# One core, long-convolution block: the forward and the inverse table product that share a matrix go into one matmul of 256 columns, the cosine products go to GpSimd, and the hand-written order is drawn up anew

## The chip, the core and the metric

The kernel runs on one core of one Trainium2 chip. A core has five engines with a queue each, and each runs its queue strictly in order: TensorE (PE: matmuls, and PEld for the weight loads in front of them), VectorE (DVE), ScalarE (ACT), GpSimd (POOL) and SyncE (SP, which only issues transfers here). Engines wait for each other through semaphores. The metric is device time in microseconds (us) of one execution, lower is better.

## The reference, cut to what matters

The program is a sequence of two residual blocks on a 2048 x 512 input:

```python
h  = x + A(layernorm(x))        # A: a state-space convolution
h2 = h + B(layernorm(h))        # B: a gated MLP over tokens

def A(u):                       # u: (1, L=2048, D=512), N=128 states per channel
    dt = exp(log_dt); A = -exp(log_A_real) + 1j*A_imag; C = (C_real + 1j*C_imag)*dt[:, None]
    P  = exp((A*dt[:, None])[:, :, None] * arange(L))
    K  = 2.0*einsum("dn,dnl->dl", C, P).real          # one filter of length L per channel
    y  = irfft(rfft(K, 2*L) * rfft(u.T, 2*L))[:, :L]  # convolution by FFT of length 4096
    return y.T + u*D_skip

def B(x):
    z = gelu(x @ w_in); z1, z2 = split(z)
    return (z1 * (w_sp @ layernorm(z2) + b_sp)) @ w_out
```

The change touches only A: how the filters K are generated, and how they and the input go through the transform.

## The kernel before, in words

**Stages.** The program has four parts, one after the other: phase A (`phase_a`, the convolution), then `phase_b1`, `phase_b2` and `phase_b3` (block B). Phase A works through the 512 channels in four chunks of 128 (`NCH`); each chunk is cut into eight pieces of 16 channels. All its arithmetic is float32.

**A unit** (`unit`, L481; 32 of them, eight per chunk) generates the filters of 16 channels as a sum over the 128 states. PE makes phases from a table (`ps<-c_k,sw`), ACT and DVE reduce them (`wb<-ps,wb`, `wb<-wb,ps`), ACT takes the sine of both halves (`ps<-wb` of 1024 columns), the absolute value, and the cosine of both halves (two activations of 512 columns: `ce`, and `cw`, L499 to L501). POOL makes three products of decay tables (`wa<-mt`). DVE makes the three sine products (`f<-ps,wa`, `f<-wa,ps`) and the `ce` product (`wa<-ps,wa`, 1024 columns). The `cw` product is made on DVE for odd units (`wb<-ps,wa`, with `cw` in a PSUM bank) and on POOL for even ones (`wb<-wb,wa`, with `cw` in SBUF), by `EVERY = 2`. PE then sums over the states in two rounds of 16 small matmuls (`ps<-f` and `ps<-wa,wb`), and ACT or DVE copies the result to one of six buffers `ks`.

**The tables** of decays (`table`, L471) are made for a half of a chunk: POOL multiplies (`mt<-rcs,wb`), ACT takes an exponential (`mt<-mt`), POOL multiplies once more. The exponential needs another function table in ACT than sine does, so ACT loads a table ahead of it and the sine's table again behind it (`ACT_TABLE_LOAD`).

**The transform** of a chunk has five kinds of pieces:
- a (`piece_a`): first step of the transform of the input (weights `big` or `wa`, moving `c_f` in `wb`); the result goes to `x1us`, that is `trio[1]` for chunk 0 and `big[2]` for the others.
- b (`piece_b`): second step. For each of 32 frequencies a matrix of the table `a2` (`a` in the profile) is the stationary operand, and 128 columns of `x1us` move. Four frequencies fill a PSUM bank; ACT or DVE copies it to the spectrum in `trio` (`trio<-ps`, 512 columns).
- c (`piece_c`): the first step for the filters of a unit (weights `ks`); the result goes to `x1k`, that is `big[3]`.
- d (`piece_d`): the second step for the filters, with the same 32 matrices of `a2`. DVE multiplies the result into the spectrum (`trio<-ps,trio`, 1024 columns: the PSUM bank is read for two planes). For chunks 0 to 2 there are eight groups of four matrices with 128 columns; for chunk 3 the 32 lanes are cut in two halves (`split`, L645), so that there are two times four groups of eight matrices with 64 columns.
- e (`piece_e`): the inverse step (weights `trio`, moving `c_inv`), copied to `big`, from which block B begins (matmuls `y<-big,g`).

`exchange(c)` swaps the halves of a spectrum with two transfers (`trio<-trio`), after the inverse step of chunk c-1 has read them.

**What sets the order.** In phase A nothing is issued as it is written. Every operation is recorded by `Plan`; the string `RANKS` gives each a rank, `FORMS` chooses between two engines where `either` leaves the choice (mostly PSUM copies on ACT or DVE), `BANKS` names the PSUM bank. Then all are issued by rank from one helper, which is why they all have the line L250, each engine's queue in that order. A matmul in float32 stands as two records in the profile.

## Time and profile before

| what | value |
|---|---|
| median of 3 runs | 848.29 us (847.11 to 849.35) |
| the profiled execution: its own time | 844.69 us |
| its span | 842.9 us, granted clock 0.999 |
| busy over the span | PE 794.1 us, PEld 685.6 us, DVE 654.2 us, ACT 469.1 us, POOL 278.5 us |
| last copy of phase A starts | 296.76 us |
| first matmul of block B starts | 297.40 us |

The span is what the engines show from their first instruction to their last; the execution's own time is 1.8 us more. "Busy" is the union of an engine's instructions. For PE that includes their pipeline: records overlap, so what one costs is the length of a run of records divided by their number, not the mean of one. A group's row in the profile ends with the engine's idle time ahead of it and what ended that.

### The profile page before, as it was taken

The numbers are of one execution on the slowest core, as the hardware profiler recorded it, in microseconds if no ns is written. First come the engines' busy times: TensorE is split into PE (matmuls) and PEld (weight loads), VectorE is DVE, ScalarE is ACT, GpSimd is POOL, SyncE is SP. The second block draws the span as 40 slices with busy tenths as digits, with TensorE's granted clock in tenths as the row PEclk, the third lists the DMA queues.
The fourth block names the chain that finished last, engine by engine and source line by source line (L and its number), as shares of the span: only waits on it lengthen the run. The fifth ranks groups of instructions, "written<-read, shape, count | busy, mean of one in ns | idle before, by whom it ended". The sixth has DMA issues, their size and how long they took to land.

```text
span 842.9 us, 17463 instructions
## 1 busy us (share of the span) xinstructions
PE 794.1 (94%) x6813; PEld 685.6 (81%) x6813; DVE 654.2 (78%) x1260; ACT 469.1 (56%) x783; POOL 278.5 (33%) x332
## 2 busy tenths in 40 slices
PE   1388999999998999999999999999999999999998
PEld 0287889899997998888899988888887888888886
DVE  7999998999999488851367679988955985787633
ACT  5998999999897233543223345456534533454111
POOL 5778777787755000000042100324221002222200
PEclk9999999999999999999999999999999999999999
DMA  9231432302218676364175044899889558799832
GB/s 352 76 113 32 111 91 61 86 25 62 52 38 269 233 251 163 99 172 154 51 150 126 1 126 132 187 228 213 201 206 210 171 149 189 156 236 216 204 110 77
DMA packets 63875, 121.81 MB, mean 145 GB/s; under 512 B 6737, under 2 KB 21201, under 8 KB 61489
## 3 DMA queue, kind: packets, MB, share of 16 engines
q1 hardware_dynamic: 52160, 99.33, 38.9%
q0 software_dynamic: 11632, 21.37, 15.6%
q8 instruction: 53, 0.87, 0.4%
q14 instruction: 30, 0.24, 0.1%
HBM read 92.89 MB, written 19.40 MB: 133 GB/s over the span
## 4 chain that ended last, share of the span: by engine, by line
PE 67%; DVE 14%; DMA 7%; issue 6%; ACT 5%; POOL 1%; SPq 1%; DVEq 0%; ACTq 0%; POOLq 0%
PE ps L250 20%; PE m L1140 18%; PE pz L835 9%; PE pz L935 9%; DMA raws<-in_w_sp_dram 6%; PE po L1063 5%; DVE trio L250 4%; PE y L748 3%; PE pl L1063 2%; ACT wb L250 2%; DVE wts L676 1%; ACT big L250 1%; ACT ps L250 1%; DVE wb L250 1%; DVE f L250 1%
## 5 line engine op out<-in xcount | busy, mean ns | idle before, releaser
L1140 PE MATMUL m<-wts,zc_wa 128*128 128x512 f32 x700 | 218.0, 391 | 1.0 <-DVE c L1155 1.0
L1140 PEld LDWEIGHTS m<-wts,zc_wa 128*128 128x128 f32 x700 | 131.4, 188 | 29.8 <-DVE c L1155 1.5
L1140 PE MATMUL m<-wts,zc_wb 128*128 128x512 f32 x350 | 136.7, 391 | 0.0
L1011 POOL DMA_DIRECT2D raws<-in_w_sp_dram x64 | 58.1, 1009 | 209.2 <-DMA raws<-in_w_sp_dram 208.0
L250 POOL TENSOR_TENSOR wa<-mt 128x512 f32<-128x512 f32 x96 | 107.3, 1131 | 35.2 <-PE ps L250 15.6
L675 ACT CAST wts<-raws 128x512 fp32r<-128x512 f32 x112 | 68.8, 619 | 52.3 <-DMA raws<-in_w_sp_dram 31.7
L676 DVE TENSOR_TENSOR wts<-raws,wts 128x512 fp32r<-128x512 f32 x112 | 77.0, 690 | 19.6 <-ACT wts L675 19.5
L935 PE MATMUL pz<-w,ht 128*128 128x448 f32 x384 | 77.4, 363 | 0.0
L1140 PEld LDWEIGHTS m<-wts,zc_wb 128*128 128x128 f32 x350 | 65.7, 188 | 14.0
L935 PEld LDWEIGHTS pz<-w,ht 128*128 128x128 f32 x384 | 72.0, 188 | 5.3
L835 PE MATMUL pz<-ht,w1h 128*128 128x512 f32 x224 | 71.3, 395 | 0.0
L250 ACT ACTIVATE ps<-wb 128x512 f32<-128x512 f32 (+1 forms) x80 | 65.3, 825 | 3.4 <-DVE trio L250 1.3
L941 POOL TENSOR_SCALAR sm<-sm 128x1 f32<-128x1 f32 x16 | 5.5, 342 | 186.3 <-DVE sm L940 186.3
L250 PE MATMUL ps<-big,a 128*128 128x128 f32 (+1 forms) x512 | 62.4, 278 | 0.9 <-DVE trio L250 0.8
L675 ACT CAST zc_wa<-raws 128x384 fp32r<-128x384 f32 (+1 forms) x70 | 37.0, 533 | 46.8 <-DVE raws L1045 34.1
L1063 PE MATMUL po<-w,gz 128*128 128x512 f32 x252 | 62.6, 396 | 0.0
L250 PEld LDWEIGHTS ps<-big,a 128*128 128x128 f32 x512 | 59.3, 192 | 3.5 <-DVE trio L250 1.1
L250 PE MATMUL ps<-c_inv,trio 128*128 128x128 f32 x512 | 60.6, 277 | 1.3 <-DVE trio L250 1.3
L250 PEld LDWEIGHTS ps<-c_inv,trio 128*128 128x128 f32 x512 | 58.8, 192 | 3.2 <-DVE trio L250 1.9
L1063 PEld LDWEIGHTS po<-w,gz 128*128 128x128 f32 x252 | 47.3, 188 | 11.5 <-DVE zo L1103 0.4
L835 PEld LDWEIGHTS pz<-ht,w1h 128*128 128x128 f32 x224 | 42.1, 188 | 9.2
L1045 DVE TENSOR_TENSOR raws<-z 128x384 f32<-128x384 f32 (+1 forms) x80 | 46.1, 584 | 0.3
(162 smaller groups left out, 1533.0 us busy)
## 6 DMA issues: line engine op xcount, KB each, us to landing
raws<-in_w_sp_dram SPq DMA_DIRECT2D x112, 256.0 KB, 4.0
raws<-in_w_sp_dram POOLq DMA_DIRECT2D x80, 256.0 KB, 5.8
trio<-trio SPq DMA_DIRECT2D x8, 1024.0 KB, 6.9
g<-in_c_g_dram SPq DMA_DIRECT2D x8, 1024.0 KB, 6.7
scr_z<-zo SPq DMA_DIRECT2D x28, 256.0 KB, 2.3
big<-in_u_a_dram SPq DMA_DIRECT2D x8, 512.0 KB, 7.6
xq<-in_u_b_dram SPq DMA_DIRECT2D x4, 1024.0 KB, 6.7
scr_h<-xq SPq DMA_DIRECT2D x16, 256.0 KB, 4.9
```

Of the source, the lines that this page charges most:

```text
L250: r = getattr(getattr(self.nc, e), method)(*map(self.real, args), **{k: self.real(x) for k, x in kw.items()})
L675: nc.scalar.copy(hi, src)
L676: nc.vector.tensor_sub(lo, src, hi.bitcast(F32))
L748: nc.tensor.matmul(ys[n, g][:, i, :], gt[:, i, r, :], qv[:, r, l0 + i], start=(r == 0), stop=(r == 1))
L835: nc.tensor.matmul(pt, w[:, q, f], ht[n][k][:, q], start=(q == 0 and i == 0), stop=(q == 3 and i == 2))
L935: nc.tensor.matmul(pt[:, :FQ], a[:, q], w2[:, b, q, f], start=(q == 0 and i == 0), stop=(q == 3 and i == 2))
L941: nc.gpsimd.tensor_scalar_add(sm[:, 14:15], sm[:, 13:14], 1e-5)
L1011: nc.gpsimd.dma_start(r, ws[1], accum_op=ALU.add)
L1045: nc.vector.tensor_tensor(zs[:, :w], x, y, op=op)
L1063: nc.tensor.matmul(pt, gz[fb][x][:, P * a:P * a + P], wo[:, y, fb, w], start=(first and fb == fbs[0] and i == 0), stop=(last and fb == fbs ...
L1140: nc.tensor.matmul(pt, x[:, f], y, start=(k == 0 and i == 0), stop=(k == KT - 1 and i == 2))
```

## The change

Phase A alone is changed, in four places.

1. Piece b of chunk c+1 and piece d of chunk c become one piece `piece_bd(c, g)` for c = 0, 1, 2: one matmul per frequency with 256 moving columns (128 of `x1us` and 128 of `x1k`, which lie side by side in `big[2:4]`). Two frequencies fill a bank, so there are 16 groups in place of 8 + 8; each group is emptied by one copy of 256 columns (ACT or DVE) and one DVE product of 512 columns. `piece_b` stays for chunk 0, `piece_d` for chunk 3. To fit, `x1us` takes the layout of `x1k`.
2. Chunk 3's piece d is no longer cut in halves: eight groups of four matrices with 128 columns, as the other chunks had.
3. The `cw` product is made on POOL for all units; `cw` stays in SBUF.
4. `RANKS`, `FORMS` and `BANKS` are new strings.

```diff
-            ce, cw = nc.bank([P, 1, W], 0), nc.bank([P, W], 0) if su % EVERY == 1 % EVERY else cs[:, 0, :]
-            nc.scalar.activation(ce, cs[:, 1:2, :], AF.Sin, bias=half_pi, scale=-TWO_PI)
-            nc.scalar.activation(cw, cs[:, 0, :], AF.Sin, bias=half_pi, scale=-TWO_PI)
+        ce, cw = nc.bank([P, 1, W], 0), cs[:, 0, :]
+        nc.scalar.activation(ce, cs[:, 1:2, :], AF.Sin, bias=half_pi, scale=-TWO_PI)
+        nc.scalar.activation(cw, cs[:, 0, :], AF.Sin, bias=half_pi, scale=-TWO_PI)
...
-        if su % EVERY == 1 % EVERY:
-            nc.vector.tensor_mul(cs[:, 0, :], cw, m[:, 2, :])
-        else:
-            nc.gpsimd.tensor_tensor(cw, cw, m[:, 2, :], op=ALU.mult)
+        nc.gpsimd.tensor_tensor(cw, cw, m[:, 2, :], op=ALU.mult)
         with nc.group():
-            product(cs[:, 0, :], m[:, 0:2, :], 1)
+            product(cw, m[:, 0:2, :], 1)
...
-    x1us = [x.rearrange("p (k d q) -> p k d q", k=NK1, q=4) for x in (trio[:, 1], big[:, 2, :])]
+    x1us = [x.rearrange("p (k q d) -> p k q d", k=NK1, q=4) for x in (trio[:, 1], big[:, 2, :])]
+    x1b = big[:, 2:4, :].rearrange("p i (k q d) -> p i k q d", k=NK1, q=4)
...
+    def piece_bd(c, g):
+
+        pt = bank("s2", [P, 2, 32, 2, 4])
+        with nc.group():
+            for j in range(2):
+                nc.tensor.matmul(pt[:, :, :, j, :].rearrange("p i d q -> p i q d"), a2v[:, 2 * g + j, :], x1b[:, :, 2 * g + j, :, :],
+                                 start=True, stop=True)
+        o = spectra(c + 1)[0][:, :, 2 * g:2 * g + 2, :]
+        nc.either(lambda: nc.scalar.copy(o, pt[:, 0]), lambda: nc.vector.tensor_copy(o, pt[:, 0]))
+        v = spectra(c)[2].rearrange("p i (d k) -> p i d k", d=32)[:, :, :, 8 * g:8 * g + 8]
+        nc.vector.tensor_mul(v, pt[:, 1].rearrange("p d k q -> p d (k q)").unsqueeze(1).to_broadcast([P, 2, 32, 8]), v)
...
         if c + 1 < NCH:
             pieces(piece_a, c + 1)
-            pieces(piece_b, c + 1)
-        split = [(0, 32)] if c + 1 < NCH else [(0, 16), (16, 16)]
-        for lo, m in split:
-            for g in range(NK1 // (1 << (P // m).bit_length() - 1)):
-                piece_d(c, g, lo, m)
-            for s in range(lo // 4, (lo + m) // 4):
-                piece_e(c, s)
+        for g in range(16 if c + 1 < NCH else 8):
+            if c + 1 < NCH:
+                piece_bd(c, g)
+            else:
+                piece_d(g)
+        for s in range(8):
+            piece_e(c, s)
```

Of the three strings one line each shows the kind of change:

```diff
-    "05000608010709040B0F0A0R0M0V0I0f0Z0j03020C0E0G0H0J0K0L0O0Q0S0U0X0Y0a0N0b0d0m0g0l0o0r0u0z10121316181A1D1Y1O1a1d1h1t221w25"
+    "07000504010Q060B0A0F0I090M080b0k0W0g03020C0E0G0H0J0K0L0N0O0R0U0V0Z0c0Y0d0e0m0i0l0p0r0v0y0z0-11121416191K1U1X1r1p1w252629"
```

What they do to the queues shows at three places. The first is the end of phase A on PE: the last pieces of chunk 3 (c from `ks`, d from `big,a`, e from `c_inv`). Before:

```order
L250 MATMUL ps_101<-big,a_78 128x4x16 x8
L250 MATMUL ps_100<-big,a_78 128x4x16 x8
L250 MATMUL ps_103<-big,a_78 128x4x16 x8
L250 MATMUL ps_98<-big,a_78 128x4x16 x8
L250 MATMUL ps_102<-f_94 32x64 x16
L250 MATMUL ps_102<-wa,wb 32x64 x16
L250 MATMUL ps_100<-f_95 32x64 x16
L250 MATMUL ps_100<-wa,wb 32x64 x16
L250 MATMUL ps_102<-wb,ks_80 64x128 x8
L250 MATMUL ps_100<-wb,ks_81 64x128 x8
L250 MATMUL ps_101<-c_inv,trio 128x128 x8
L250 MATMUL ps_103<-c_inv,trio 128x128 x8
```

and at the same place now, from the last two units on:

```order
L250 MATMUL ps_101<-f_94 32x64 x16
L250 MATMUL ps_101<-wa,wb 32x64 x16
L250 MATMUL ps_103<-wb,ks_85 64x128 x8
L250 MATMUL ps_99<-wb,ks_80 64x128 x8
L250 MATMUL ps_102<-f_95 32x64 x16
L250 MATMUL ps_102<-wa,wb 32x64 x16
L250 MATMUL ps_103<-wb,ks_83 64x128 x8
L250 MATMUL ps_101<-wb,ks_81 64x128 x8
L250 MATMUL ps_100<-big,a_78 128x4x32 x4
L250 MATMUL ps_102<-big,a_78 128x4x32 x4
L250 MATMUL ps_103<-big,a_78 128x4x32 x4
L250 MATMUL ps_101<-big,a_78 128x4x32 x4
```

Before, the first half of piece d stood ahead of the last two units and the second half stood among the inverse pieces; now all of piece d stands behind the last piece c, and the eight inverse pieces behind it, with nothing else between.

The second place is PE at the passage from chunk 0 to chunk 1. Now the merged pieces stand in one run behind the last piece c (`ks_81`) of chunk 0:

```order
L250 MATMUL ps_103<-wb,ks_84 64x128 x8
L250 MATMUL ps_102<-wb,ks_81 64x128 x8
L250 MATMUL ps_100<-ident,trio 128x128
L250 MATMUL ps_103<-big,a_78 128x2x4x32 x2
L250 MATMUL ps_102<-big,a_78 128x2x4x32 x2
L250 MATMUL ps_100<-big,a_78 128x2x4x32 x2
L250 MATMUL ps_99<-big,a_78 128x2x4x32 x2
```

where before the same run held piece d alone, and piece b of chunk 1 (`128x128`) had been done earlier, between the units:

```order
L250 MATMUL ps_103<-wb,ks_81 64x128 x8
L250 MATMUL ps_102<-wb,wa 64x128 x8
L250 MATMUL ps_100<-big,a_78 128x4x32 x4
L250 MATMUL ps_103<-big,a_78 128x4x32 x4
L250 MATMUL ps_102<-big,a_78 128x4x32 x4
L250 MATMUL ps_100<-big,a_78 128x4x32 x4
L250 MATMUL ps_99<-big,a_78 128x4x32 x4
```

The third place is ACT where the decay tables of chunk 1 are made. Before, each half of a chunk had its exponential alone, with a table load on either side:

```order
L250 ACTIVATE wb<-wb 128x512
L250 ACT_TABLE_LOAD
L250 ACTIVATE mt_92<-mt_92 128x2176
L250 ACTIVATE wb<-ps_98,wb 128x1024
L250 ACT_TABLE_LOAD
L250 ACTIVATE ps_100<-wb 128x512
```

and now both halves stand within one pair of loads:

```order
L250 ACT_TABLE_LOAD
L250 ACTIVATE mt_93<-mt_93 128x2176
L250 COPY trio<-ps_103 128x32x8
L250 ACTIVATE ps_101<-ps_101 128x256
L250 ACTIVATE mt_92<-mt_92 128x2176
```

The load of the sine's table follows 14 rows later, behind the copies of the merged pieces. Over phase A ACT issues 11 table loads, 18 before.

More of the change, by code (lines that the diff above doesn't have):

```diff
@@ L28 @@
 WIDE = 2
-EVERY = 2
 SUC = 8
@@ new lines @@
+    "2B2D2H0x2G0+102I2L2Z2Q2V2S2o2d2m2j1Z1l2X3N3e3p0P0D0X0T0h0S0a0n0q350j1M2u0t18131W3t361G1P1d1u3w1Y1b1e1h1a1g1f1c0u0o0w1T0f"
+    "1I1V1i1j1H1F1A1D171C151O1R1S1k1J1N1m1L1o1v1z24271-2A2E2J2K2M2N2P2R2T2U2W2Y2a2b2c2s2g2-3A3H313f2n343E2e333l2k3M3W3Q3Z3d37"
+    "2v2r3B3J2p2+2q2i3P30452x2l322f3T1y3V3X1B1s2z1E3F383K3I2C3R3L233D0s2F1n1q2w2t3C221Q3O202y21391x3Y3c3g3i3o3j3q3u3x3+404142"
+    "43444647484A4D4C4E4F4N4J5c4j525G4M4Q4-4o4k4G4Z4m5d5J5D4P4H4K4I4Y4b4L544c5S4R4p4U584h4O5i5n5m67652h3h3n3r3y4d4f4l4n4v4q4w"
@@ L631, in phase_a @@
     pieces(piece_a, 0)
-    pieces(piece_b, 0)
+    for g in range(8):
+        piece_b(g)
     exchange(0)
```

86 lines of the change are left out of this document (39 added, 47 removed).

## The prediction

> **What bounds the kernel now.** The change is in phase A alone, so I first looked where phase A ends and whether its end moves what follows. The chain of work that ended last, in order of time (start, length, what):
>
> ```profile
> 274.97 21.72 PE ps L250 x192
> 296.76 0.59 ACT big L250
> 297.40 9.20 PE y L748 x80
> ```
>
> Phase A ends with 192 PE records without a gap, one copy, and block B's first matmul at 297.4 us; from there the chain is PE again. Block B is not changed, so what phase A gains or loses should reach the end whole. Next, the busy time of PE, PEld, DVE, ACT and POOL in three stretches of phase A (bounds in us, length, then busy us and instructions):
>
> ```profile
> 44.00:107.00 63.00, 59.14 (x1087) 52.27 (x1087) 61.19 (x102) 59.43 (x95) 48.61 (x57) 1.00 0.35 93
> 107.00:273.00 166.00, 162.02 (x2924) 147.16 (x2922) 157.94 (x203) 151.90 (x190) 116.94 (x124) 1.00 0.32 83
> 273.00:297.40 24.40, 23.28 (x222) 22.84 (x218) 11.21 (x11) 7.36 (x13) 0.21 (x1) 1.00 0.56 209
> ```
>
> Up to 107 us DVE is the fullest, 61.2 of 63. From 107 to 273 PE is, 162.0 of 166, with DVE at 95% and ACT at 92%; POOL has 70%. The last 24 us are PE alone. The granted clock is full throughout. So three engines are nearly full together, and no term can be taken at its own size without asking what the other two do.
>
> **The change part by part.**
>
> *PE.* What a record costs is read from unbroken runs (start, length, count at the end):
>
> ```profile
> 219.59 8.20 PE L250 MATMUL ps<-big,a 128*128 128x128 f32 x72
> 263.03 7.36 PE L250 MATMUL ps<-big,a 128*128 128x64 f32 x64
> 320.38 5.58 PE pz L835 x24
> ```
>
> 128 columns cost 8.20/72 = 0.114 us a record, and 64 columns 7.36/64 = 0.115: half the columns save nothing. A float32 matmul is two records. Chunks 0 to 2 lose 2 x 32 matmuls each, 384 records, 43.7 us, and get 32 of 256 columns each, 192 records. That record is not in the trace. How long a record lasts grows with its columns, though:
>
> ```profile
> L250 PE MATMUL ps<-wb,ks 128*64 128x128 f32 x512 | 32.1, 275 | 0.7 <-DVE big L250 0.5 <-DVE wa L250 0.2
> L250 PE MATMUL ps<-f 128*32 128x64 f32 x1024 | 20.8, 222 | 2.1 <-DVE big L250 1.1 <-DVE wa L250 0.8 <-DVE f L250 0.2
> ...
> L935 PE MATMUL pz<-w,ht 128*128 128x448 f32 x384 | 77.4, 363 | 0.0
> L835 PE MATMUL pz<-ht,w1h 128*128 128x512 f32 x224 | 71.3, 395 | 0.0
> ```
>
> In phase A 64 more columns add 275 - 222 = 53 ns, 0.83 ns a column; in block B (rounded operands, one record a matmul) 395 - 363 = 32 ns, 0.5 ns. So a float32 record pays nearly double for a column, and 256 of its columns are like 512 of block B's, in a run 5.58/24 = 0.233 us. Below, 256 x 0.83 = 0.212 bounds it; above, two records of 128 columns, 0.228, are close by, and the run itself is the upper end. I take 0.233, the nearest row: 192 x 0.233 = 44.7 us, **+1.0 us** (at 0.212: -3.0). The merge itself saves PE nothing.
> [...]
>
> Chunk 3 loses 64 matmuls of 64 columns (128 records, 14.7 us) for 32 of 128 columns (64 records, 7.3 us): **-7.4 us**. This is the largest certain term, and it lay on PE's path: 64 of those records are the run at 263.03, ahead of the last two units. But they also were cover. At the end of phase A:
>
> ```profile
> 271.43 3.48 DVE L250 TENSOR_TENSOR trio<-ps,trio 128x1024 f32<-128x1024 f32 x3
> 272.60 1.97 PE L250 MATMUL ps<-wb,ks 128*64 128x128 f32 x32
> 287.52 9.15 PE L250 MATMUL ps<-c_inv,trio 128*128 128x128 f32 x80
> ```
>
> From the end of the last piece c (274.57) to block B (297.40) were 22.8 us. Now all of piece d stands there: a copy 0.6, the first group 0.9, then eight DVE products that start (3.48 - 1.22)/2 = 1.13 us apart, 9.0 (PE needs only 0.92 a group and waits), 128 inverse records at 9.15/80 = 0.114, 14.6, a copy 0.6: 25.8 us, **+3.0 us**. Nothing is left to fill PE's wait there.
>
> *DVE, ACT and POOL.* The forms' rows (busy us, mean ns):
>
> ```profile
> L250 DVE TENSOR_TENSOR f<-ps,wa 128x512 f32<-128x512 f32 x64 | 41.9, 683 | 1.3 <-ACT ps L250 1.1
> L250 DVE TENSOR_TENSOR trio<-ps,trio 128x1024 f32<-128x1024 f32 x32 | 37.4, 1218 | 9.4 <-PE ps L250 9.1
> L250 ACT ACTIVATE ps<-wb 128x512 f32<-128x512 f32 x48 | 32.5, 689 | 1.6 <-DVE trio L250 0.6 <-DVE wa L250 0.4
> L250 ACT ACT_TABLE_LOAD x18 | 23.1, 1283 | 1.0 <-PEq L1246 0.7
> L250 POOL TENSOR_TENSOR wb<-wb,wa 128x512 f32<-128x512 f32 x16 | 20.5, 1280 | 13.6 <-ACT wb L250 13.3 <-DVE big L250 0.2
> L250 POOL TENSOR_SCALAR big<-big,trio 128x96 f32<-128x96 f32 x27 | 18.9, 784 | 3.1 <-DVE trio L250 3.1
> L250 ACT ACTIVATE big<-big,trio 128x96 f32<-128x96 f32 x37 | 15.7, 542 | 1.9 <-DVE trio L250 1.9
> L250 ACT ACTIVATE wb<-wb 128x512 f32<-128x512 f32 x16 | 11.5, 718 | 0.2
> L250 DVE TENSOR_TENSOR wb<-ps,wa 128x512 f32<-128x512 f32 x16 | 10.9, 684 | 0.6 <-ACT ps L250 0.5
> L250 ACT COPY trio<-ps 128x512 f32<-128x512 f32 x19 | 10.8, 583 | 1.9 <-PE ps L250 1.7
> L250 DVE COPY ks<-ps 128x256 f32<-128x256 f32 x16 | 6.7, 418 | 0.6 <-PE ps L250 0.6
> L250 ACT COPY ks<-ps 128x256 f32<-128x256 f32 x16 | 5.9, 371 | 7.3 <-PE ps L250 7.0
> L250 POOL TENSOR_TENSOR trio<-trio 128x128 f32<-128x128 f32 x7 | 3.1, 449 | 3.2 <-ACT trio L250 2.8 <-POOL mt L250 0.4
> ```
>
> DVE: 24 products of 1024 columns become 48 of 512, priced like the `f` products: 48 x 0.683 - 24 x 1.218 = +3.6. Sixteen `cw` products go: -10.9. By the new order it has one 512-column copy more (+0.7, as the `f` rows), as many of 256 columns, and five small products fewer (about -1.5). Sum **-8.1 us**.
> ACT: counted from the two orders, 74 copies of 512 columns become 49 (-25 x 0.583 = -14.6), 16 of 256 columns become 64 (+48 x 0.371 = +17.8); sixteen cosines are written to SBUF at 0.718 instead of 0.689 (+0.5); five copies of the layer norm go to POOL (-2.7); and seven table loads vanish (-7 x 1.283 = -9.0), which the four-part description doesn't say and only the order shows. Sum **-8.0 us**.
> POOL: sixteen `cw` products at 1.28 (+20.5), five norm copies (+3.9), five small products (about +2.5). Sum **+26.9 us**, against 117 + 49 us of work in the 229 us from 44 to 273; it would be busy 84% where it was 72%.
>
> *What of this reaches the end.* From 107 us on PE sets the pace: -7.4 + 1.0 + 3.0 = -3.4 us. DVE and ACT fall by more than PE does, so neither becomes the bound through its own sum. Before 107 us DVE sets the pace, and PE stands idle for 63 - 59.1 = 3.9 us; with `cw` products gone from DVE, and chunk 1's pieces b moved behind the eighth unit, I take half of that idle time as gained: -2.0 us (ends: 0 and -3.9). Together -5.4, say **-5.5 us**. The cost of the new order itself, how well the queues mesh, has no row: I take 0, and bound it by what waits there can be: POOL's, below (+10), and the whole excess of DVE's and ACT's sums over PE's (-8).
>
> *Waits added or moved.* The merged pieces must follow all eight units of their chunk, so chunk c+1's piece b no longer fills gaps between units. While 16 groups run (16 x 4 x 0.233 = 14.9 us), no other PE work stands between; DVE needs 16 x 0.683 = 10.9 and ACT about 16 x 0.371 = 5.9 of that, so both can work ahead on two or three units (three `f` and `cs` buffers). The exchange of chunk 3 starts when the last inverse piece of chunk 2 has run, and its two transfers go one after the other:
>
> ```profile
> 256.21 0.46 SPq L250 DMA_DIRECT2D trio<-trio  x1
> trio<-trio SPq DMA_DIRECT2D x7, 1024.0 KB, 6.9
> ```
>
> 14 us in all, ahead of the first product of piece d; in the new order four units and all eight pieces c stand between on PE, about 18 us by DVE's rows. It should just be covered; without that cover it costs up to the difference, a few us. SP's loads for block B stand behind it as before, some 36 us ahead of their use.
>
> **The rivals.**
>
> *A: POOL becomes the pace (slower).* POOL's waits between 40 and 275 us (total, times, longest):
>
> ```profile
> POOL wa L250 <- PE ps L250: 15.6, 13, 2.6
> POOL wa L250 <- DVE wb L250: 13.9, 11, 2.6
> POOL wb L250 <- ACT wb L250: 13.3, 8, 4.5
> POOL ks L250 <- ACT ks L250: 10.2, 6, 3.9
> ```
>
> These 53 us are not free time but latency: POOL may not refill a buffer before PE has read it, and has two of them. If they stay as they are, 26.9 us of new work lengthens phase A by up to that; if the new work replaces them, by nothing. It decides from 8.0 us on, three tenths of the new work, that isn't absorbed: then the -5.5 is used up and 2.5 us (0.3%) stand on top. For half unabsorbed: +13.4 - 5.5 = +7.9, some 852.6 us in the profiled execution. For it: the third product of each unit now stands behind 1.28 us more on a strict queue. Against: POOL's share stays under DVE's and ACT's of before.
>
> *B: it cancels (no change).* The merged run and the tail leave PE idle as long as the saved records took: the gain ahead of 107 us doesn't come (2.0), and the three merged runs each cost about 1 us at their ends, where units' matmuls waited for by DVE and ACT stand behind 14.9 us of them. For it: PE and DVE were both full there, so the run can't be hidden. Against: both are relieved. -5.5 + 2.0 + 3 = -0.5, some 844 us in the profiled execution.
>
> *C: the three sums are realised (much faster).* If the path in phase A is shared by PE, DVE and ACT in turn, what counts is that all three fall by 7 to 8 us, and the tail's +3.0 is partly hidden: -10 to -13, about 833 us.
>
> **How the numbers follow.** The profiled execution took 844.69 us, 3.6 less than the median of the runs shown, 848.29; I apply the differences to the median. Forecast -5.5 (between -2.5 and -9): 842.8 us, chance 0.47. C, -11.5: 836.8, chance 0.19. B, -0.5: 847.8, chance 0.19. A, +7.9: 856.2, chance 0.15, of which half lies under +5. The range leaves out the outer half of A and the outer part of C: 835 to 853. A measurement of this kernel can tell about 0.3% (2.5 us) from no change; so faster 0.66, same 0.20, slower 0.14 (part of A is that small).
>
> **What would show it.** In the changed profile: records of 256 columns in runs of about 0.23 us each; 11 table loads in phase A; DVE about 8 us less busy before the last piece c; POOL's waits for PE, DVE and ACT shorter by most of 27 us; the last stretch from the last piece c to block B 25 to 26 us, with PE waiting for DVE in piece d; block B starting near 292. If POOL's rows stand at the head of the chain in the stretches of units, A was right; if PE idles ahead of or behind the merged runs, B. The forecast is wrong if the 256-column record costs clearly more or less than 0.233, or if block B takes another length than before.

## The result, and the profile after

The changed kernel is **slower by 1.5%**: 861.79 us median of 13 executions (853.48 to 865.93) against 848.29 for the kernel before (844.38 to 853.44); the ratio is 1.0154, with a 95% interval of 1.0124 to 1.0185. The forecast was 842.8 us, the range 835 to 853. The profiled execution took 853.48 us, the least of its 13, 8.8 us more than the profiled one of before; all positions below are from such profiles.

The first part of the page of the changed kernel, and its groups of instructions with shapes kept apart:

```profile
PE 789.7 (93%) x6557; PEld 671.2 (79%) x6557; DVE 649.3 (76%) x1263; ACT 458.2 (54%) x795; POOL 303.6 (36%) x358
```

```profile
L250 POOL TENSOR_TENSOR wa<-mt 128x512 f32<-128x512 f32 x96 | 106.9, 1132 | 3.8 <-PE ps L250 2.3 <-DVE f L250 0.2 <-POOL ks L250 0.2
L250 PE MATMUL ps<-big,a 128*128 128x256 f32 x192 | 43.8, 384 | 2.0 <-ACT trio L250 1.1 <-ACT big L250 0.4 <-DVE trio L250 0.4
...
L250 POOL TENSOR_TENSOR wb<-wb,wa 128x512 f32<-128x512 f32 x32 | 41.0, 1283 | 26.3 <-ACT wb L250 26.3
L250 DVE TENSOR_TENSOR trio<-ps,trio 128x512 f32<-128x512 f32 x48 | 32.2, 687 | 11.9 <-PE ps L250 6.2 <-ACT trio L250 5.3
...
L250 ACT ACT_TABLE_LOAD x11 | 14.1, 1283 | 0.9 <-PEq L1251 0.7
```

The sums moved the way that was forecast: against before PE is 4.4 us less busy, DVE 4.9, ACT 10.9 with its 11 table loads, POOL 25.1 more. Less work on three engines, and yet a longer kernel. The chain that ended last, at the end of phase A (start, length, what), shows the first place:

```profile
272.48 1.02 PE ps L250 x35
273.49 4.56 issue
278.06 3.29 PE ps L250 x29
281.37 0.59 ACT big L250
282.01 1.17 PE ps L250 x8
...
286.61 5.75 DVE trio L250 x5
292.40 14.29 PE ps L250 x126
306.69 0.35 issue
307.04 0.59 ACT big L250
307.68 2.39 PE y L753 x19
```

Block B starts at 307.68, where before had 297.40: +10.3 us. PE stops for 4.56 us at 273.49, and no engine releases it. The timeline of PE puts the stop in the middle of one group of equal matmuls, the last piece c, whose operands were all there:

```profile
273.06 0.43 PE L250 MATMUL ps<-wb,ks 128*64 128x128 f32 x3
278.06 3.28 PE L250 MATMUL ps<-wb,ks 128*64 128x128 f32 x29 [4.56 <-issue]
```

29 records that took 1.97 us for 32 before now take 3.28. A window there shows why (bounds, length, busy us of PE, PEld, DVE, ACT, POOL, granted clock, DMA share, GB/s), and a table of the stages of phase A shows the second place:

```profile
278.00:279.00 1.00, 0.94 (x10) 0.94 (x11) 0.00 (x0) 0.00 (x0) 0.00 (x0) 0.50 1.07 451
```

```profile
96.05:114.70 18.65, 16.36 (x70) 12.48 (x72) 13.64 (x28) 11.21 (x19) 11.66 (x13) 1.00 0.08 22
114.70:162.59 47.89, 45.48 (x917) 38.83 (x915) 46.35 (x65) 45.90 (x63) 43.73 (x46) 1.00 0.40 93
162.59:176.85 14.26, 14.26 (x66) 12.10 (x68) 9.62 (x14) 8.07 (x18) 8.41 (x9) 1.00 0.00 1
176.85:222.18 45.33, 44.16 (x912) 38.38 (x913) 43.28 (x60) 44.56 (x58) 37.90 (x40) 1.00 0.32 75
222.18:236.90 14.72, 14.35 (x64) 11.99 (x64) 10.97 (x18) 10.45 (x18) 8.08 (x8) 1.00 0.01 1
236.90:273.50 36.60, 34.24 (x749) 29.38 (x750) 35.42 (x46) 35.62 (x53) 31.19 (x33) 1.00 0.32 70
273.50:282.00 8.50, 3.28 (x29) 2.95 (x28) 0.69 (x1) 0.64 (x2) 0.21 (x1) 0.80 1.00 415
282.00:307.70 25.70, 21.99 (x193) 21.61 (x193) 16.27 (x17) 3.96 (x6) 0.00 (x0) 1.00 0.53 207
```

The rows of 18.65, 14.26 and 14.72 us are the merged runs, those of 47.89, 45.33 and 36.60 the units between them. In the merged runs DVE is busy 34.2 of 47.6 us and ACT 29.7; in the units 125.1 and 126.1 of 129.8, 96 and 97%, with PE at 123.9, 95%. Work that was mixed now stands apart: in the merged runs PE is full and the others wait, and in the units all three are full. A count of PE's records says the same. When the matrices of d of chunk 1 and b of chunk 2 are done, at 181.07 us, the kernel before has made 576 of its 1024 `ps<-f` records, two units more than the 512 of the chunks so far. In the changed kernel the same point comes at 176.81 us, with exactly 512: no unit stands ready.

The positions used from here on, in us (the start of the last record of a chunk's last piece c, block B's first matmul, and the time from the end of the last c to it):

```
                      c of chunk 0,1,2     c of chunk 3   block B   between
before                109.8 169.8 218.8       274.3        297.4     22.8
after                  95.1 161.6 221.2       281.0        307.7     26.3
e1_again               96.4 162.9 222.5       280.8        309.5     28.3
e2_cw_back                        232.2       293.0        325.1     31.7
e3_late_loads                                 282.6        314.7     31.6
e4_cw_alone                                   280.2        302.8     22.4
e5_warm_tail                                  286.5        314.5     27.6
e6_short_exchange                             279.5        307.7     28.0
e7_merged_reordered                           295.0        323.4     28.0
e8_before_reordered                           290.2        308.3     17.9
e9_half_merged                                274.5        302.9     28.0
e9_half_before                                275.3        298.4     22.8
e10_no_lock                                   280.3        312.1     31.4
e11_both               95.3 161.8 221.5       274.8        303.0     28.0
e12_shared_tail                               274.1        300.9     26.5
e13_filled_tail                               274.7        302.1     27.2
e14_half_and_cw                               279.3        300.6     21.0
e15_before_cw_packets                         277.4        300.0     22.4
e16_sine_before                               277.8        300.5     22.4
e17_all_three                                 273.7        296.3     22.4
```

### The profile page after: what moved, and what is told of

Same layout as the page of the kernel before. It is cut to its first block, busy times and chain, and to the rows that moved or that the text cites. A ratio compares the mean times of both kernels' runs of the same rounds, so it can differ in the third digit from the quotient of the medians.

```text
span 851.7 us, 17003 instructions
## 1 busy us (share of the span) xinstructions
PE 789.7 (93%) x6557; PEld 671.2 (79%) x6557; DVE 649.3 (76%) x1263; ACT 458.2 (54%) x795; POOL 303.6 (36%) x358
## 4 chain that ended last, share of the span: by engine, by line
PE 76%; DVE 14%; POOL 3%; issue 3%; ACT 2%; DMA 2%; SPq 0%; DVEq 0%; POOLq 0%
PE m L1145 32%; PE ps L250 13%; PE pz L840 9%; PE pz L940 9%; PE po L1068 7%; DVE trio L250 4%; PE y L753 3%; DVE f L250 3%; DVE wa L250 2%; PE pl L1068 2%; POOL wa L250 2%; DVE big L250 2%; DVE wb L250 2%; DMA big<-in_u_a_dram 2%; POOL wb L250 1%
## 5 line engine op out<-in xcount | busy, mean ns | idle before, releaser
L250 ACT ACTIVATE wb<-wb 128x1024 f32<-128x1024 f32 (+1 forms) x64 | 56.4, 887 | 0.6
L250 ACT ACTIVATE ps<-wb 128x1024 f32<-128x1024 f32 (+1 forms) x64 | 54.6, 858 | 2.6 <-DVE wb L250 1.7
L250 PE MATMUL ps<-big,a 128*128 128x256 f32 (+1 forms) x256 | 51.2, 357 | 2.7 <-ACT trio L250 1.1
L250 DVE TENSOR_TENSOR trio<-ps,trio 128x512 f32<-128x512 f32 (+2 forms) x58 | 41.9, 746 | 14.6 <-PE ps L250 8.9
L250 PEld LDWEIGHTS ps<-big,a 128*128 128x128 f32 x256 | 42.9, 190 | 10.9 <-ACT big L250 2.6
```

The lines of the kernel that those rows point to most:

```text
L250: r = getattr(getattr(self.nc, e), method)(*map(self.real, args), **{k: self.real(x) for k, x in kw.items()})
```

## The experiments

Ratios are to the kernel before on the same chip, with 95% intervals.

**1. Is it POOL's product?** First the changed kernel once more. Then two runs on the `cw` product: in the changed kernel half of the products back on DVE, and in the kernel before all of them on POOL and nothing else changed. In the expectations theory P is rival A, theory U the mechanism of rival B, and theory F the stop of PE.

> The changed kernel once more, unaltered, for a second profile and as the control of the next three. Its first profile is the fastest of its runs (853.5 us against a median of 861.8). Theory F (PE runs out of code while block B's first loads fill the DMA engines, then finds its clock halved): this profile shows stops of PE in the middle of a group of equal matmuls, longer or more of them than the 4.56 us at 273.5, with stretches of granted clock 0.5 behind them, and these make up the 8 us between the two. Theory U (merged pieces and units take turns instead of overlapping) and theory P (POOL, with all cosine products, sets the pace) expect the units' stretches themselves to be longer than in the first profile. Time: 861.8, ratio to before 1.015.

857.84 us, ratio 1.0147 [1.0098, 1.0197]: the loss is there again. The stop is not longer than in the first profile (3.75 us against 4.56), so it does not make the difference between the fastest execution and the median, as theory F had it.

```diff
# e2_cw_back, on the changed kernel
-        nc.gpsimd.tensor_tensor(cw, cw, m[:, 2, :], op=ALU.mult)
+        if su % 2:
+            nc.vector.tensor_mul(cw, cw, m[:, 2, :])
+        else:
+            nc.gpsimd.tensor_tensor(cw, cw, m[:, 2, :], op=ALU.mult)
# e4_cw_alone, on the kernel before (and `cw` in SBUF for all units)
...
-        if su % EVERY == 1 % EVERY:
-            nc.vector.tensor_mul(cs[:, 0, :], cw, m[:, 2, :])
-        else:
-            nc.gpsimd.tensor_tensor(cw, cw, m[:, 2, :], op=ALU.mult)
+        nc.gpsimd.tensor_tensor(cw, cw, m[:, 2, :], op=ALU.mult)
```

> Changed kernel, but the cosine product of odd units back on DVE (16 x 0.68 us there, 16 x 1.28 us off POOL). Theory P: POOL's 20.5 us go, 8 to 13 us faster than the changed kernel. Theory U: in the units' stretches DVE is 95 to 97% busy and POOL about 90%, so DVE's 10.9 us count at half or more: 4 to 8 us slower than the changed kernel, about 867.

> Kernel before, its order and pieces untouched, with the cosine product of odd units on POOL (the one part of the change that can be made alone). Theory P: slower by 5 us or more (853 and up). Theory U: POOL has room between the pieces there, within 3 us of before.

e2_cw_back: 868.94 us, 1.0254 [1.0221, 1.0287]. Sixteen products on DVE (10.9 us) put the last c 12 us later. e4_cw_alone: 848.88 us, 1.0017 [0.9995, 1.0038]. So POOL can carry the products, and rival A falls as the cause of the loss: taking POOL's new work off makes it worse. In the new order DVE's time in the units is worth its full size; in the old order the same 10.9 us are worth nothing that shows. e4's profile has two stops of PE in it (1.97 and 1.56 us), and e15 below makes the same move with small packets.

One sign that the prediction named for A is there all the same. Of the chain that ended last, POOL's rows hold 51% between 236.9 and 273.5 us, the third stretch of units, in the profiles of after and of e1; in the first two stretches they hold 2 and 13%, and in e11 below 10% of the third. POOL is thus as near to being the bound there as DVE is; giving it less work at DVE's expense doesn't help.

**2. The stop of PE.** The profiles have a DMA queue `q8 instruction`: 53 packets of 16 KB before, 51 in the changed kernel. PE's matmuls and weight loads are 13626 and 13114, 257 to a packet in both, so these packets are read here as PE's code. The DMA view of two windows of the changed kernel, 267.8 to 275.8 and 275.8 to 276.9 us (queue, packets, MB, share of the 16 engines):

```profile
DMA packets 239, 2.11 MB, mean 264 GB/s; under 512 B 29, under 2 KB 29, under 8 KB 29
q1 hardware_dynamic: 239, 2.11, 90.6%
...
DMA packets 57, 0.46 MB, mean 417 GB/s; under 512 B 2, under 2 KB 2, under 8 KB 2
q1 hardware_dynamic: 56, 0.44, 100.4%
q8 instruction: 1, 0.02, 5.3%
```

For 8 us no code packet runs, while the exchange of chunk 3 (whose 16 KB packets take 1.28 us each) and block B's loads keep the 16 DMA engines 90.6% busy. The theory is that PE ran out of code. The places of the stops bear it out. If one counts PE's instructions in the profile, weight loads and semaphore instructions included, from 0 on, PE goes on after this stop with number 7617. Between 40 and 320 us the 20 profiles hold 36 stops of PE of over 0.4 us that no engine releases, and every one of them ends at a number that leaves 193 or 194 when divided by 256. A wait for data would have no reason to keep to such places. That code comes in blocks of 256 instructions is inferred from them and from the 257 to a packet. The instruction 256 places ahead of the stop ran at 268.82; the next packet starts at 275.85, 7.0 us later, and takes 0.94; at 278.06 PE goes on.

In the changed kernel there are two shorter stops of this kind, 1.41 us at 83.1 and 0.42 at 89.8. They are not in e11 below, and chunk 0's last c comes there at 95.3 as against 95.1: those two cost nothing that shows.

What keeps the code packet waiting, the exchange or the loads? Two runs: one that was to hold the loads back until the last c is done, and one with an exchange of chunk 3 that moves an eighth (in packets of 2 KB).

```diff
# e3_late_loads: block B's loads to wait for the copy of the last piece c
+        e = evac(x1k[:, :, :, 4 * s:4 * s + 4], pt.rearrange("p d q k -> p k q d"))
+        if c + 1 == NCH and s == 7:
+            final.append(e)
...
+                if o is final[0]:
+                    loads(o["ins"].name)
...
+        tc.add_manual_dep(load_x(0).ins, name, info, reason="after the last piece c")
+        for _ in range(2):
+            load_g(sg, "g")
...
# e6_short_exchange
-        one = nc.sync.dma_start(b[:64], a[64:])
-        two = nc.sync.dma_start(b[64:], a[:64])
+        n = 32 if c < 3 else 4
+        one = nc.sync.dma_start(b[:64, :n], a[64:, :n])
+        two = nc.sync.dma_start(b[64:, :n], a[:64, :n])
```

> Changed kernel, but block B's first loads (xq, g, w1r) are issued only behind the last piece c of chunk 3; nothing else moves. Theory F: the stop of 4.56 us and the half clock behind it go (about 6 us in the profile), and the median falls by at least as much, to 850 to 856. Theories U and P: nothing moves, 860 to 863; if the loads then come too late, slower.

> Changed kernel, but the exchange of chunk 3 moves 4 of the 32 lanes only (an eighth of the two transfers of 1 MB; the rest of that exchange is left out). Block B's loads stay where they are. Theory F, sharper after the late loads changed nothing: PE's code fetch stands behind the exchange's packets on its DMA engine. Then the stop of about 4 us in the middle of a group at 273 to 275 us goes or falls under 1.5 us, the clock stays full, the last piece c ends near 277 instead of 281, and the median falls by 5 to 8 us, to 851 to 855. If the fetch is late for the loads or for another reason: the stop stays near 4 us and the median within 2 us of the changed kernel.

e3_late_loads: 860.11 us, 1.0162 [1.0115, 1.0208], a stop of 4.03 us. This run doesn't decide, though: the wait is put on the first load alone, and the queue of SP shows the other eight issued ahead of the last c (282.6) as before, from 268.9 on where after has 266.8:

```profile
268.92 2.71 SPq L716 DMA_DIRECT2D g<-in_c_g_dram  x2
272.42 1.42 SPq L711 DMA_DIRECT2D xq<-in_u_b_dram  x1
274.52 1.94 SPq L726 DMA_DIRECT2D w1r<-in_w_dram  x4
276.50 7.52 SPq L711 DMA_DIRECT2D xq<-in_u_b_dram  x2
```

(The last row holds the eighth of them, at 276.50, and the one that was held back, at 283.69.) e6_short_exchange: 855.53 us, 1.0091 [1.0059, 1.0123]. PE's timeline:

```profile
276.55 0.43 PE L250 MATMUL ps<-wb,ks 128*64 128x128 f32 x3
277.95 1.80 PE L250 MATMUL ps<-wb,ks 128*64 128x128 f32 x29 [0.97 <-issue]
```

The same records, the same place, and 0.97 us in place of 4.56, with block B's loads where they were. So the exchange makes most of the stop; the 0.97 us left may be the loads', which no run tests alone. PE goes on 1.2 to 1.6 us after the code packet has ended, however long it stood, at all 36 stops; six of them:

```
                    code packet: start, took    PE goes on
after                    275.85   0.94            278.06
e1_again                 276.13   0.93            278.55
e3_late_loads            277.17   0.91            279.69
e5_warm_tail             281.23   0.94            283.63
e6_short_exchange        275.57   1.06            277.95
e10_no_lock              275.14   0.96            277.33
```

Two profiles (e5, e6) showed something else near 56 us: one DVE instruction of 128x128 that takes 4.22 and 3.92 us; one of the same shape takes 0.22 at 51.99 in before. In e5's timelines of DVE and of POOL:

```profile
55.93 4.22 DVE L250 TENSOR_SCALAR trio<-trio 128x128 f32<-128x128 f32 x1
```

```profile
55.53 1.29 POOL L250 TENSOR_TENSOR wb<-wb,wa 128x512 f32<-128x512 f32 x1
56.76 3.31 POOL L250 TENSOR_TENSOR wa<-mt 128x512 f32<-128x512 f32 x3
```

It lasts from within POOL's cosine product to the end of the three products behind it; in after's profile it took 0.57. In these two profiles chunk 0's last c comes at 101.4 and 98.8 us, against 95.1 to 96.4 in after and e1, and nothing of that is made up later. I moved this instruction to POOL (e10), and in a second run also cut each half of the exchange into eight transfers, so that its packets have 2 KB in place of 16 (e11, for every chunk).

```diff
# e10_no_lock
-        nc.vector.tensor_scalar(b, cr, 0.0, 2.0, op0=ALU.is_lt, op1=ALU.mult)
+        (nc.gpsimd if c0 == 1 else nc.vector).tensor_scalar(b, cr, 0.0, 2.0, op0=ALU.is_lt, op1=ALU.mult)
# e11_both: that, and (the second half waits for the first, as before)
-        one = nc.sync.dma_start(b[:64], a[64:])
-        two = nc.sync.dma_start(b[64:], a[:64])
+        for o, i in ((slice(0, 64), slice(64, 128)), (slice(64, 128), slice(0, 64))):
+            with nc.group():
+                for lo in range(0, 32, 4):
+                    nc.sync.dma_start(b[o, lo:lo + 4], a[i, lo:lo + 4])
```

> Changed kernel; one small DVE operation of the parameters of chunk 1 (tensor_scalar of 128 columns, 0.22 us, from SBUF to SBUF) is made on POOL. In the profiles of 858.6 and 851.9 us span it took 4.2 and 3.9 us, until POOL's cosine product and three decay products behind it had ended; in the others 0.5 to 0.8. Theory L (this is what parts the changed kernel's runs into 853 to 857 and 860 to 866): no such stretch, hardly a run over 860, the median falls by 4 to 7 us, to 854 to 858. If the spread has another cause: median 860 to 863 as before.

> Changed kernel with the same operation on POOL, and every exchange cut into eight transfers of 128 KB a half (packets of 2 KB instead of 16 KB). Theories L and F: the code fetch at 268 us gets in between the packets, the stop of about 4 us falls under 2, and both together bring 8 to 12 us: 850 to 854. If smaller packets let no fetch through: as with that operation on POOL alone.

e10_no_lock: 857.28 us, 1.0131 [1.01, 1.0163]. The longest of its four executions took 858.92 us, where the changed kernel without it had some of up to 867.94 (e1), but the median is not to be told from e1_again's, so the worth of this edit stays open. e11_both: **850.4 us, 1.0037 [1.0012, 1.0062]**. PE's timeline of e11 has the group whole again:

```profile
272.54 0.65 PE L250 MATMUL ps<-wa,wb 128*32 128x64 f32 x32
273.12 1.97 PE L250 MATMUL ps<-wb,ks 128*64 128x128 f32 x32
```

The code packet starts 1.5 us after the same instruction has run (268.84 to 270.36), there is no stop and no half clock at it, and the last c comes at 274.8, not 280.3 as in e10. The cut of the exchange is all that was changed between these two, but it changes two things. SP now issues sixteen transfers in place of two, and block B's loads, which stand behind them in its queue, start 6.7 us later. In e10 and in e11:

```profile
259.56 7.22 SPq L250 DMA_DIRECT2D trio<-trio  x2
266.87 0.61 SPq L707 DMA_DIRECT2D xq<-in_u_b_dram  x1
```

```profile
259.72 13.70 SPq L250 DMA_DIRECT2D trio<-trio  x16
273.53 0.52 SPq L713 DMA_DIRECT2D xq<-in_u_b_dram  x1
```

Which of the two, the smaller packets or the later loads, lets the code packet through isn't separated.

**3. The tail.** Behind the last c PE waits for DVE, as forecast, but in some profiles the clock then falls too. Two windows of e11:

```profile
283.20:286.20 3.00, 0.03 (x1) 0.03 (x1) 2.92 (x3) 0.00 (x0) 0.00 (x0) 0.99 0.99 412
286.20:289.60 3.40, 3.40 (x16) 3.40 (x17) 0.00 (x0) 1.29 (x2) 0.00 (x0) 0.51 1.04 408
```

3 us without PE work, then 3.4 us at half the clock. It isn't so each time: the same wait, of 2.9 to 3.0 us, has half clock at its end in e2, e3, e6, e10 and e11, and none in after, e1 and e9_half_merged. e5 makes the first of the four matmuls of each group of piece d twice; e12 gives two of d's eight products to ACT and POOL; e13 puts 12 matmuls whose result nobody reads ahead of an inverse piece (and gives it another bank).

```diff
# e5_warm_tail, on the changed kernel
-            for j in range(4):
+            for j in (0, 0, 1, 2, 3):
# e12_shared_tail, on e11
+        if g in (2, 3):
...
+            nc.scalar.copy(t, pt.rearrange("p d k q -> p d (k q)"))
+            nc.gpsimd.tensor_tensor(v, t.unsqueeze(1).to_broadcast([P, 2, 32, 16]), v, op=ALU.mult)
...
# e13_filled_tail, on e11
+            for _ in range(12 if (c, s) == (3, 4) else 0):
+                nc.tensor.matmul(pt[:, 0, :], a2v[:, 0, :], x1k[:, 0, :, :], start=True, stop=True)
```

> Changed kernel; in chunk 3's piece d the first of the four matmuls of each group is made twice (8 matmuls, 16 records, about 1.8 us of PE that wait for DVE's products anyway). Theory C (the halved clock in the tail, where PE waits for DVE between the groups of piece d, makes the difference between 853 and 862 us): the halved stretches behind the last units get shorter, the last stretch stays at 25 to 27 us in the profile, and the median falls by 3 to 6 us, to 853 to 857. If the clock falls for the stop of PE at 273 us alone, and not for the tail: within 2 us of the changed kernel (858 to 862).

> As the kernel with both remedies (850.4 us; in its profile 28.2 us from the last piece c to block B, PE waits 2.98 us for DVE in piece d, then 3.4 us at half clock), but two of the eight products of piece d of chunk 3 are made by an ACT copy and a POOL product. The last stretch falls to 24 to 25.5 us, PE waits under 1.7 us, no half clock there; the median falls by 3 to 4.5 us, to 846 to 847.5. If the tail is not what is left: 850.

> As the kernel with both remedies, but 12 more matmuls of 128 columns (24 records, 2.8 us) between piece d and the first inverse piece of chunk 3, where PE waits for DVE; their result is overwritten. If the clock is halved for that wait: the clock stays full in the last stretch, which falls from 28.2 to 25 to 26.5 us, median 847.5 to 849. If the wait alone counts: 850 to 851.

e5_warm_tail: 863.41 us, 1.019 [1.0155, 1.0225], no gain; the stop is in it as well, and the DVE instruction of 4.22 us. e12_shared_tail: 848.51 us, 1.001 [0.9986, 1.0034]; e13_filled_tail: 848.4 us, 1.0 [0.9975, 1.0025]. Both profiles keep the full clock (26.5 and 27.2 us in place of 28.0), and both are level with the kernel before, not better; their intervals overlap e11's. In e13 PE's wait falls to 0.69 us. In e12 it is still 2.85 us, so that its full clock may be chance. Part of what DVE gained there it lost at the first product of piece d, which waits for the exchange:

```profile
277.49 3.49 DVE L250 TENSOR_TENSOR trio<-ps,trio 128x1024 f32<-128x1024 f32 x3 [3.16 <-DMA trio<-trio]
```

That wait comes with the small packets. The exchange ends at 277.2 us in e12, while the two large transfers of the changed kernel had landed by 273.0 (issued at 266.2, 6.7 us to landing).

**4. What sets the pace of the units?** Without stop and half clock the changed kernel only reaches the old position: e11 to e13 have the last c at 274.1 to 274.8, before 274.3. The forecast's gain of 8.4 us ahead of it is missing. So I left out PE work: half of the merged matmuls in the changed kernel (21.3 us), and half of those of the pieces b and d in the kernel before (21.9 us).

```diff
# e9_half_merged, on the changed kernel: piece_bd
-            for j in range(2):
+            for j in range(1):
# e9_half_before, on the kernel before: piece_b, piece_d
-            for j in range(4):
+            for j in range(4 if c == 0 else 2):
...
-            for j in range(kn):
+            for j in range(kn // 2 if c + 1 < NCH else kn):
```

> Changed kernel; of the two matmuls of each merged group only the first is made (48 of 96 merged matmuls left out: 96 records of 0.222 us, 21.3 us of PE; copies and DVE products stay). Theory U (the merged runs are PE's alone and fully on the path, the units' stretches are paced by DVE, ACT and POOL together): at least 10 us faster than the changed kernel, 845 to 852. If PE's time in these runs is covered: within 4 us of the changed kernel.

> Kernel before; the same work left out there (half of the matmuls of pieces b of chunks 1 to 3 and of pieces d of chunks 0 to 2: 192 records of 0.114 us, 21.9 us of PE). The prediction's reading, PE sets the pace from 107 us on: most of it shows, 15 to 20 us faster than before, 828 to 833. Theory U (there these pieces lie between units that wait for DVE, ACT and POOL anyway): less than 6 us faster, 842 to 848.

e9_half_merged: 854.28 us, 1.0084 [1.0049, 1.0118], some 6 us for 21.3; its profile has stops of 1.7 and 4.7 us and 17 us at half clock in it, so the work left out may be worth more than that. e9_half_before: 846.89 us, **1.0016 [0.9996, 1.0035]: with 21.9 us of PE's work left out nothing is gained**. Two stops (1.05 and 1.10 us) and 3.4 us at half clock, in its profile and not in before's, can hide at most 4 us of a gain. The windows' sums over 44 to 273 us, of the kernel before and of e9_half_before:

```profile
sum 229.00, PE 221.16 PEld 199.44 DVE 219.14 ACT 211.33 POOL 165.55; mean PE 55.29 PEld 49.86 DVE 54.78 ACT 52.83 POOL 41.39
```

```profile
sum 229.00, PE 206.79 PEld 180.58 DVE 218.00 ACT 211.06 POOL 165.48; mean PE 51.70 PEld 45.14 DVE 54.50 ACT 52.76 POOL 41.37
```

PE is 14.4 us less busy in the same 229 us; of the 7.5 us missing, half clock explains at most 1.7 (3.4 us, in the first window). The chain that ended last tells who took over. Between 107 and 273 us PE's rows hold 72% of it in the kernel before, and 39% in e9_half_before, where DVE's and ACT's together have grown from about a quarter to over half. DVE, 95.7% busy, was the next suspect, then ACT. On the kernel before: e4's edit and the small packets (e15); both of these and half of b's and d's matmuls (e14); ACT's sine shortened (e16, 26 us); all three (e17).

```diff
# e16_sine_before
-        nc.scalar.activation(ph, cs, AF.Sin, scale=-TWO_PI)
+        nc.scalar.activation(ph[:, :, :32], cs[:, :, :32], AF.Sin, scale=-TWO_PI)
```

> Kernel before with all cosine products on POOL and exchanges in packets of 2 KB, nothing left out. Alone, the products on POOL gave 848.9, with stops of PE of 2.0 and 1.6 us in the middle of groups and 6.8 us at half clock in the profile. If code fetch behind the exchange made these: they go, 843 to 846, a little faster than before. If not: 848 to 849.

> Kernel before with all cosine products on POOL (DVE 10.9 us less), half of the matmuls of pieces b of chunks 1 to 3 and d of chunks 0 to 2 left out (PE 21.9 us less), and exchanges in packets of 2 KB. If PE and DVE hold the pace together: 10 us or more faster than before, under 838. If ACT (92% busy, untouched here) and the order hold it as well: 842 to 847.

> Kernel before; the sine of each unit is taken of 64 of its 1024 columns only (the rest left out): 32 ACT operations of 1.03 us fall to about 0.2, some 26 us of ACT. If ACT alone sets the pace of the units: 10 us or more faster, under 838. If ACT shares it with PE and DVE, or the order holds it: 2 to 6 us faster at most, 842 to 848.

> The same on top of half of the matmuls of pieces b and d left out, all cosine products on POOL and exchanges in small packets: PE 21.9, DVE 10.9, ACT 26 us less than before. If the three full engines hold the pace together: 12 us or more faster than before, under 836. If even that gives under 5 us, the pace is set by how the queues wait for one another (the chain of a unit through the engines, at three buffers), not by any sum: 843 to 848.

e15: 848.11 us, 0.9999 [0.9974, 1.0023]. e14: 847.06 us, 0.9991 [0.9963, 1.0019]. e16: 848.7 us, 1.003 [1.0004, 1.0056]. e17: 843.95 us, 0.9968 [0.9948, 0.9988]. e17's sum over the same windows:

```profile
sum 229.00, PE 208.77 PEld 182.53 DVE 212.06 ACT 187.94 POOL 185.94; mean PE 52.19 PEld 45.63 DVE 53.02 ACT 46.99 POOL 46.48
```

No engine is over 93% busy, and 2.7 us are gained. Stops are absent from this profile; 6.8 us at half clock (0.97 in two of e17's windows) cloud it by 3.4 us at most. So the sums of PE, DVE and ACT, cut by 21.9, 10.9 and some 26 us, don't set the pace, alone or together. What is left is how the four strict queues wait for one another: the order, with the few buffers that it has. That is inferred from what was ruled out. POOL's own work, up to 81% of these windows, was not cut in any run, and none has more buffers.

Small packets are no cure by themselves: e15 keeps one of e4's two stops, with 0.99 us in place of 1.56. There the code packet came early, 1.2 us after the instruction 256 places ahead, but PE was through with the block in 2.6 us.

**5. Another order.** If the order is the cause, one drawn anew from measured durations might help. Both kernels got new `RANKS`, `FORMS` and `BANKS`, from the durations in their profiles, and nothing else.

> Changed kernel with the same pieces, all cosine products on POOL, but another order (ranks, PSUM copies and banks drawn up anew: units stand ready around and inside the merged runs, inverse pieces spread between units, the exchanges away from the densest code). Theory U (units and merged runs take turns; it is the order that lost the gain): 10 to 18 us faster than the changed kernel, 842 to 850, with DVE and ACT idle for less than half of the 13 and 15 us beside the merged runs. Theory P (POOL's added work): POOL's work is the same, so 856 or more.

> Kernel before, pieces untouched, its order drawn up anew in the same way as for the changed kernel with a new order. Tells what the order alone is worth with the old pieces, so what the merge is worth in an order that suits it. Theory U: 839 to 846, and 2 to 6 us above the merged pieces in their new order. If the old order was already as good as it gets: 846 to 849.

Both are slower, where a gain was expected: e7 872.36 us, 1.0296 [1.0268, 1.0324], with stops of PE of 1.2 to 5.3 us in the middle of groups and 20 us at half clock; e8 858.7 us, 1.0139 [1.0106, 1.0172], the kernel before made 1.4% slower by its order alone (two stops of 0.6 and 1.4 us and 6.8 us at half clock are in its profile). So an order drawn from durations can cost as much as the whole loss here. They don't show that a good order would bring the forecast's gain.

## Why the prediction was wrong

**The step that failed is "From 107 us on PE sets the pace".** On it rested -7.4, +1.0 and, with the -2.0 ahead of 107 us, all of the -8.4 up to the last c. PE was 98% busy there, but that share is no price: e9_half_before takes away three times as much of PE's work (in chunks 0 to 2, where the -7.4 lies in chunk 3) and gains nothing. DVE's -8.1 and ACT's -8.0 were counted as making room; e14, e16 and e17 show that in the old order they were no price either, or 2.7 us for all three.

**"The cost of the new order itself ... I take 0, and bound it by what waits there can be: POOL's, below (+10)".** The bound was of the right size (9 us, below), with the wrong place (POOL's waits). Between blocks of PE time and of DVE and ACT time the work no longer overlaps: "both can work ahead on two or three units" fell short, for in the merged runs DVE is idle 13.4 of 47.6 us. The longest wait of POOL shows how the far end stands still:

```profile
POOL wb L250 <- ACT wb L250: 23.0, 10, 10.8
```

One wait of 10.8 us, for a cosine that ACT makes only behind its copies of the merged run.

**What nobody priced is the code.** The forecast said that the exchange "should just be covered" and looked only at DVE's wait for it. That part was right: in the changed kernel the exchange had landed by 273.0 us, ahead of the first product of piece d even without the stop (277.0 in e11). In the profiled execution it was, by the place of the stop and by e6 (0.97 us in place of 4.56), PE's code that stood behind it: +6.2 us with the half clock after the stop (281.0 against 274.8 in e11).

The books of the profiled execution, from the last c: forecast -8.4, measured +6.8 (its end 281.35 against 274.57). Of these 15.2, 6.2 are the stop, and 9 the gain that never was, by e11 to e13. Behind it the tail has 26.3 us where 25.8 was forecast. Block B is 1.5 us shorter (544.0 against 545.5), for no reason that I looked into. The median is 4.7 us further off than this execution. Half clock in the tail gives part of that (28.3 and 31.4 us in e1 and e10), the long DVE instruction near 56 us perhaps another (chunk 0's last c is 6.3 and 3.7 us later in the two profiles that have it); how much each is worth in the median stays open.

**Right were** the counts, the direction of the sums (ACT -10.9 for -8.0, POOL +25.1 for +26.9, 11 loads; DVE -4.9 for -8.1 was the furthest off), POOL's waits giving way to its new work, and the tail's +3.0 (+3.5), with PE's wait for DVE in it (5.75 us of DVE in the chain). The record of 256 columns was mis-sized. PE's timeline of the second and the third merged run:

```profile
162.59 14.22 PE L250 MATMUL ps<-big,a 128*128 128x256 f32 x64
222.18 12.35 PE L250 MATMUL ps<-big,a 128*128 128x256 f32 x56
```

14.22/64 = 0.222 and 12.35/56 = 0.2205, inside the bounds but under the 0.233 taken: the merge saves PE about 1.2 us where the sum had +1.0.

**The rivals.** A fell with e2 and e4 as the cause, though its sign shows in the third stretch of units. C fell: the sums were realised and brought nothing. B had the mechanism, merged runs that can't be hidden and a gain ahead of 107 us that doesn't come. The first two merged runs end 3.9 and 4.3 us ahead of the same matrices in the kernel before (114.6 and 176.8 us against 118.5 and 181.1), but with one and two units fewer made, at some 6 us a unit (47.89/8). e11 is near B's kernel in size (+0.4% for its -0.1%); B lacked the stop.

## What to carry to other kernels

A busy share of 98% is not a price. Take work of that engine out of the old kernel first: one run here would have shown that leaving out 21.9 us of it gains nothing. When work that filled gaps is gathered into one long run, count what the other engines can do meanwhile, and expect them to be the bound in what is left. And where an unrolled stream of instructions passes a long DMA of large packets, look for stops in the middle of a group of equal instructions that no engine releases. Here they lie a multiple of 256 instructions apart, and an exchange in smaller packets, with the loads behind it later, took them away (e11 to e13).

## What of the hardware was not expected

- PE stood without code, as the traces are read here. The packet of 16 KB came 7.0 us after PE had begun on the 256 instructions ahead of it, and PE stopped for 4.56 us; with packets of 2 KB in the exchange it came after 1.5 us and PE didn't stop (e11). That PE lacked code is read from the places of all 36 stops, alike by 256 instructions, and from the constant 1.2 to 1.6 us behind the packet; that the exchange makes most of the long stop is shown by e6 (0.97 us); what its packet size does alone is not.
- After a wait of about 3 us the granted clock was 0.5 for 3.4 us in e11, so a wait can cost more than its length. After the same wait it stayed full in after, e1 and e9_half_merged. What decides isn't known.
- One small instruction of DVE took 4.22 us beside POOL in e5 and 3.92 in e6, and 0.57 in after. In e5 DVE stood in it through the end of POOL's cosine product and three more POOL instructions, 55.93 to 60.15 us. No run isolates it, and none shows what held it.
